# Decode attention on one core: taking the maximum of a head across partitions with two fp32 TensorE products instead of VectorE copies and transposes

## Chip, cores and metric

The kernel runs on one core of one Trainium2 chip. The metric is the time of one execution on the device in microseconds (us).

## The reference

Two attention blocks decode one token each. A has 32 heads with their own K and V of 32768 keys; B has 32 query heads over 8 K/V heads and looks at the last 4096 keys only. Cut to A, which is nearly all of the work:

```python
# A: x (1,1,512), k_cache and v_cache (1,32,32768,128), all bf16
q = (x @ wq).reshape(B, Sq, H, Dh).transpose(0, 2, 1, 3)
scores = jnp.einsum("bhqd,bhkd->bhqk", q, k_cache) * (Dh ** -0.5)
p = softmax(scores, axis=-1)
o = jnp.einsum("bhqk,bhkd->bhqd", p, v_cache)
a = o.transpose(0, 2, 1, 3).reshape(B, Sq, H * Dh) @ wo
# ... B the same with a window; out = concatenate([a, b], axis=-1)
```

One head of A reads 8.39 MB of K and 8.39 MB of V. The core reads 570 MB in all, and each byte is used once.

## The kernel before

A head of A goes through five steps. TensorE transposes K in tiles of 128 keys (`psT`) and VectorE copies them to SBUF (`kt`). TensorE multiplies them with q, so that the 32768 scores of the head stand in one PSUM bank `S` of 128 partitions by 512 (in 16 of each 32 rows, 64 in all). The maximum of the bank is taken. ScalarE computes Exp with that maximum as its bias. TensorE transposes the result (`psPT`) and multiplies it with V (PV). SyncE issues the loads; each waits for the room that it fills.

The part that the change replaces is the maximum. It takes the maximum of each row, transposes the column of 128 maxima in 32x32 blocks, copies the four pieces to one partition, takes their maximum, copies it back to four partitions, transposes again and scales:

```python
def emit_stats(self, name, g):
    self.emit_S(self.pending.pop(0))
    # ... (cut: short names; W = 16 and HG = 1 for A)
    o = dve(lambda v: v.reduce_max(tr["in"][:, 0:1], self.S[:, :], axis=AXX), self.sdone, self.k_pool)
    o = dve(lambda v: v.transpose(tr["a"][:, :], tr["in"][:, :]), o)
    for c in range(STRIPS):
        x = dve(lambda v, c=c: v.tensor_copy(m4[0:1, W * c:W * c + W], tr["a"][32 * c:32 * c + 1, 0:W]), o)
    o = dve(lambda v: v.reduce_max(t["mr"][0:1, :], m4[0:1, 0:4 * W].rearrange("p (k h) -> p h k", h=HG), axis=AXX), x)
    for c in range(STRIPS):
        x = dve(lambda v, c=c: v.tensor_copy(
            t["b"][32 * c:32 * c + 1, 0:W].rearrange("p (k h) -> p k h", k=KC),
            t["mr"][0:1, :].unsqueeze(1).to_broadcast([1, KC, HG])), o)
    o = dve(lambda v: v.transpose(t["cm"][:, :], t["b"][:, :]), x)
    o = dve(lambda v: v.tensor_scalar_mul(t["nb"][:, k:k + 1], t["cm"][:, 0:1], -self.SCALE), o, to="act")
    self.sread = self.op("act", lambda s: s.activation(
        out=self.psb[:, :], in_=self.S[:, :], func=ACTF.Exp, bias=t["nb"][:, k:k + 1], scale=self.SCALE,
        accum_out=t["oc"][k][:, DH:DH + 1]), o, self.psread, to="pe")
```

`load_v(g)` goes out when PV of head g-1 has ended (one V buffer). `load_k(g+1)` goes out when the first half of head g's K has been transposed (K has one and a half buffers). Both are on one queue, in this order. The output matrix Wo is loaded last, into the room of the last K: B's in two pieces, A's in four of 12, 10, 6 and 4 tiles of 128x512.

```python
WO_CUTS = {"A": (0, 12, 22, 28, 32), "B": (0, 16, 32)}

def emit_proj(self):
    # B's projection: 32 products into S
    for part in range(len(self.WO_CUTS["B"]) - 1):
        o = self.proj_part("B", part, ...)
    strips = self.op("dve", lambda v: v.tensor_copy(self.pb[:, :], self.S[:, :]), o)
    # A's projection: 32 products, a piece at a time, each piece after its landing
    for part in range(len(self.WO_CUTS["A"]) - 1):
        last = self.proj_part("A", part, lambda a: (self.PT[0:1, :], None, a == 0, a == 31))
        if part == 0:     # the fp32 product that adds B's four strips
            o = self.op("pe", lambda e: e.matmul(self.ACC[0:1, :], lhsT=self.e32[:, 0:1], rhs=self.pb[:, :], ...))
            self.store("B", self.ACC, 512, o)
    self.store("A", self.PT, 0, last)
```

## Time and profile before

| | kernel before |
|---|---|
| time, median of 3 runs | 1331.03 us (1330.01 to 1332.43) |
| load queue busy, of 16 engines' span | 99.4% |
| TensorE / VectorE / ScalarE busy | 72% / 61% / 4% |
| one head of A in the loop | 38.8 us |
| row maximum to Exp, in a head | 3.11 us |
| TensorE waits for Exp, all heads | 127.9 us |
| TensorE waits for K of A | 123.8 us |

First the load queue and the chain of work that ended last, from the page. The line "q1" gives packets, MB and the share of 16 engines' span.

```profile
q1 hardware_dynamic: 12628, 570.43, 99.4%
...
DMA 68%; PE 28%; DVE 3%; issue 0%; ACT 0%; SPq 0%
```

The queue is busy from end to end. The chain says 68% DMA and 28% PE. The PE share is no second limit: it lies between the landing of one K and the issue of the next K, and the V load is moving in that time. The Trainium skill ("Perfetto Trace Analysis", Identifying the Most-Contended Engine) says to optimize the most contended engine first, and to judge DMA by the HBM bandwidth used rather than by busy time. Here the DMA engines move 429 GB/s on average and the load queue is busy for 99.4% of the span, and the change does not touch it.

Now one head's maximum, from the timeline (columns: start in us, duration in us, engine, line, operation, output from inputs, forms, count; in brackets the idle time of the engine before it).

```profile
648.98 0.69 DVE L522 TENSOR_REDUCE tr_in<-psS 128x1 f32<-128x512 f32 x1 [0.51 <-PE psS L505]
649.71 0.21 DVE L523 STREAM_TRANSPOSE tr_a<-tr_in 128x32 f32<-128x32 f32 x1
649.95 0.69 DVE L525 COPY m<-tr_a 1x16 f32<-1x16 f32 x4
650.68 0.21 DVE L526 TENSOR_REDUCE mr_A<-m 1x1 f32<-1x64 f32 x1
650.92 0.70 DVE L528 COPY b_A<-mr_A 1x16 f32<-1x16 f32 x4
651.66 0.21 DVE L531 STREAM_TRANSPOSE cm_A<-b_A 128x32 f32<-128x32 f32 x1
651.90 0.15 DVE L532 TENSOR_SCALAR nb_A<-cm_A 128x1 f32<-128x1 f32 x1
652.09 0.69 ACT L533 ACTIVATE psb<-psS,nb_A 128x512 bf16<-128x512 f32 x1 [35.86 <-DVE nb_A L532]
...
652.92 0.61 PE L543 MATMUL psPT<-ident,psb 128*128 128x128 bf16 x4 [4.00 <-ACT psb L533]
...
659.65 0.33 SPq L284 DMA_DIRECT2D vbuf<-in_A_v_cache_dram  x1
...
666.20 6.24 PE L483 MATMUL psT<-ident,kbuf 128*128 128x128 bf16 x64 [4.52 <-DMA kbuf<-in_A_k_cache_dram]
```

Row maximum at 648.98, Exp at 652.09: 3.11 us. TensorE sat idle for 4.00 us until Exp was done, and again for 4.52 us until K landed. The V load was issued at 659.65, while the K issued at 637.91 landed at 666.15 only: 6.5 us of the queue were left when V joined it.

Last, the end of the run, from the timeline.

```profile
1308.15 6.09 PE L571 MATMUL psACC<-vbuf,ptsb 128*4 128x512 bf16 x64 [0.69 <-ACT ptsb L546]
...
1317.15 3.29 PE L627 MATMUL psS<-kbuf,oz_B 128*1 128x512 bf16 x32
...
1320.27 2.75 PE L627 MATMUL psPT<-kbuf,oz_A 128*1 128x512 bf16 x12
...
1323.71 4.48 PE L627 MATMUL psPT<-kbuf,oz_A 128*1 128x512 bf16 x20
...
1328.23 0.68 DVE L633 CAST out_sb<-psPT 1x512 bf16<-1x512 f32 x1 [3.64 <-PE psPT L627]
```

PV of the last head, B's projection, 12 products of A's, the fp32 product (left out here), 20 more of A's, and the copy for the store follow each other without a wait for a load. A's last piece of Wo landed at 1325.27.

### The profile page before, as it was taken

The numbers are of one execution on the slowest core, as the hardware profiler recorded it, in microseconds if no ns is written. First come the engines' busy times: TensorE is split into PE (matmuls) and PEld (weight loads), VectorE is DVE, ScalarE is ACT, GpSimd is POOL, SyncE is SP. The second block draws the span as 40 slices with busy tenths as digits, with TensorE's granted clock in tenths as the row PEclk, the third lists the DMA queues.
The fourth block names the chain that finished last, engine by engine and source line by source line (L and its number), as shares of the span: only waits on it lengthen the run. The fifth ranks groups of instructions, "written<-read, shape, count | busy, mean of one in ns | idle before, by whom it ended". The sixth has DMA issues, their size and how long they took to land.

```text
span 1330.5 us, 28787 instructions
## 1 busy us (share of the span) xinstructions
PE 953.2 (72%) x13274; PEld 668.9 (50%) x13274; DVE 805.0 (61%) x1661; ACT 54.8 (4%) x167; POOL 2.0 (0%) x15
## 2 busy tenths in 40 slices
PE   3756677686767778676687867668787667868777
PEld 3544445554444555444455544446554444555452
DVE  2655566765556676555667655566765556676573
ACT  0000000000000000000000000000000000000000
POOL 0000000000000000000000000000000000000000
PEclk9868788887788888778889878888987888888788
DMA  9999999999999999999999999999999999999997
GB/s 394 429 438 429 437 428 439 431 422 439 418 435 433 437 428 431 431 439 431 433 430 439 431 433 430 439 431 433 432 437 430 435 431 428 439 435 431 428 435 322
DMA packets 12932, 570.66 MB, mean 429 GB/s; under 512 B 1522, under 2 KB 1524, under 8 KB 1780
## 3 DMA queue, kind: packets, MB, share of 16 engines
q1 hardware_dynamic: 12628, 570.43, 99.4%
q8 instruction: 12, 0.20, 0.1%
q10 hardware_dynamic: 288, 0.00, 0.0%
q14 instruction: 4, 0.03, 0.0%
HBM read 570.43 MB, written 0.00 MB: 429 GB/s over the span
## 4 chain that ended last, share of the span: by engine, by line
DMA 68%; PE 28%; DVE 3%; issue 0%; ACT 0%; SPq 0%
DMA kbuf<-in_A_k_cache_dram 65%; PE psT L483 23%; PE psS L505 3%; DMA kbuf<-in_B_k_cache_dram 3%; DVE kt L486 3%; PE psACC L571 1%; PE psPT L627 1%; PE psS L627 0%; DVE oc_A L587 0%; ACT psb L533 0%; PE psPT L543 0%; DVE tr_in L522 0%; DVE b_A L528 0%; DVE m L525 0%; SPq L284 0%
## 5 line engine op out<-in xcount | busy, mean ns | idle before, releaser
L486 DVE COPY kt<-psT 128x1024 bf16<-128x1024 bf16 x1056 | 655.3, 684 | 203.0 <-PE psT L483 201.4
L483 PE MATMUL psT<-ident,kbuf 128*128 128x128 bf16 x8448 | 577.7, 234 | 135.8 <-DMA kbuf<-in_A_k_cache_dram 123.8
L483 PEld LDWEIGHTS psT<-ident,kbuf 128*128 128x128 bf16 x8448 | 538.3, 106 | 227.8 <-DMA kbuf<-in_A_k_cache_dram 131.9
L571 PE MATMUL psACC<-vbuf,ptsb 128*4 128x512 bf16 (+1 forms) x2112 | 188.5, 534 | 22.8 <-ACT ptsb L546 22.0
L505 PE MATMUL psS<-kt,qw 128*32 128x512 bf16 x2048 | 157.6, 385 | 15.5 <-DVE kt L486 15.5
L585 DVE TENSOR_SCALAR oc_A<-psACC,hot_A 128x128 f32<-128x128 f32 x32 | 11.2, 351 | 255.5 <-PE psG L598 255.5
L571 PEld LDWEIGHTS psACC<-vbuf,ptsb 128*4 128x4 bf16 (+1 forms) x2112 | 60.8, 111 | 141.9 <-issue 96.1
L543 PE MATMUL psPT<-ident,psb 128*128 128x128 bf16 x136 | 20.5, 305 | 127.9 <-ACT psb L533 127.9
L543 PEld LDWEIGHTS psPT<-ident,psb 128*128 128x128 bf16 x136 | 11.7, 130 | 137.6 <-ACT psb L533 137.4
L533 ACT ACTIVATE psb<-psS,nb_A 128x512 bf16<-128x512 f32 x32 | 22.0, 687 | 1169.7 <-DVE nb_A L532 1169.7
L505 PEld LDWEIGHTS psS<-kt,qw 128*32 128x32 bf16 x2048 | 34.0, 95 | 58.0 <-DVE kt L486 31.4
L598 PE MATMUL psG<-oc_A,hw 128*32 128x128 f32 (+1 forms) x128 | 19.3, 227 | 52.3 <-DVE oc_A L587 52.3
L598 PEld LDWEIGHTS psG<-oc_A,hw 128*32 128x32 f32 x128 | 11.4, 109 | 62.4 <-DVE oc_A L587 55.0
L587 DVE SCALAR_TENSOR_TENSOR oc_A<-psACC,hot_A,oc_A 128x128 f32<-128x128 f32 x96 | 33.7, 351 | 3.4
L522 DVE TENSOR_REDUCE tr_in<-psS 128x1 f32<-128x512 f32 x34 | 23.5, 692 | 17.1 <-PE psS L505 17.1
L525 DVE COPY m<-tr_a 1x16 f32<-1x16 f32 (+1 forms) x136 | 22.3, 164 | 2.6
L528 DVE COPY b_A<-mr_A 1x16 f32<-1x16 f32 x128 | 21.1, 165 | 2.4
L546 ACT ACTIVATE ptsb<-psPT 128x512 bf16<-128x512 bf16 x34 | 20.3, 597 | 32.3 <-PE psPT L543 32.3
L439 PE MATMUL psACC<-x_B,vbuf 128*128 128x1 bf16 x128 | 3.6, 165 | 13.4 <-DMA x_B<-in_B_x_dram 13.4
L439 PEld LDWEIGHTS psACC<-x_B,vbuf 128*128 128x128 bf16 x128 | 3.5, 104 | 13.4 <-DMA x_B<-in_B_x_dram 13.4
L446 DVE CAST qz<-psACC 128x32 bf16<-128x32 f32 x1 | 0.2, 192 | 12.9 <-PE psACC L439 12.9
L523 DVE STREAM_TRANSPOSE tr_a<-tr_in 128x32 f32<-128x32 f32 x34 | 7.2, 212 | 1.2
(66 smaller groups left out, 87.5 us busy)
## 6 DMA issues: line engine op xcount, KB each, us to landing
kbuf<-in_B_k_cache_dram SPq DMA_DIRECT2D x2, 4096.0 KB, 32.7
vbuf<-in_B_v_cache_dram SPq DMA_DIRECT2D x2, 4096.0 KB, 23.7
kbuf<-in_A_k_cache_dram SPq DMA_DIRECT2D x2, 4096.0 KB, 22.7
vbuf<-in_B_wq_dram SPq DMA_DIRECT2D x1, 4096.0 KB, 12.3
vbuf<-in_A_wq_dram SPq DMA_DIRECT2D x1, 4096.0 KB, 32.5
kbuf<-in_B_wo_dram SPq DMA_DIRECT2D x2, 2048.0 KB, 31.8
kbuf<-in_A_wo_dram SPq DMA_DIRECT2D x1, 1536.0 KB, 27.5
kbuf<-in_A_wo_dram SPq DMA_DIRECT2D x1, 1280.0 KB, 30.2
```

What stands on the lines that cost most here:

```text
L483: inst = e.transpose(T[:, 128 * k:128 * k + 128], src[:, DH * k:DH * k + DH], self.ident[:, :])
L486: self.copies.append(self.op("dve", lambda v: v.tensor_copy(KT[:, :], T[:, :]), o, to="pe"))
L505: inst = e.matmul(self.S[32 * c:32 * c + 32, :], lhsT=win, rhs=self.kt[(bb + c // 2) % NKT][:, 512 * (c % 2):512 * (c % 2) + 512], start=b ...
L522: o = dve(lambda v: v.reduce_max(tr["in"][:, 0:1], self.S[:, :], axis=AXX), self.sdone, self.k_pool)
L525: x = dve(lambda v, c=c: v.tensor_copy(m4[0:1, W * c:W * c + W], tr["a"][32 * c:32 * c + 1, 0:W]), o)
L528: x = dve(lambda v, c=c: v.tensor_copy(t["b"][32 * c:32 * c + 1, 0:W].rearrange("p (k h) -> p k h", k=KC), t["mr"][0:1, :].unsqueeze(1).to ...
L533: self.sread = self.op("act", lambda s: s.activation(out=self.psb[:, :], in_=self.S[:, :], func=ACTF.Exp, bias=t["nb"][:, k:k + 1], scale= ...
L543: inst = e.transpose(PT[:, 128 * jj:128 * jj + 128], self.psb[:, 128 * jj:128 * jj + 128], self.ident[:, :])
L546: self.ptread = self.op("act", lambda s: s.activation(out=self.ptsb[:, :], in_=PT[:, 0:512], func=ACTF.Copy), self.psread, to="pe")
L571: inst = e.matmul(acc[32 * c:32 * c + rows, 0:512], lhsT=lhsT, rhs=rhs, start=begin, stop=end, tile_position=(0, 32 * c), skip_group_check ...
L587: o = self.op("dve", lambda v, src=src, hot=hot: v.scalar_tensor_tensor(out=oc, in0=src, scalar=hot, in1=oc, op0=ALU.mult, op1=ALU.add), p ...
L598: return self.op("pe", lambda e: e.matmul(self.G[0:32, c0 + c:c0 + c2], lhsT=win, rhs=t["oc"][g % 2][:, c:c2], start=False, stop=True, ski ...
```

## The change

The intent: the maximum should cross the partitions by two products. The first has the column of 128 row maxima as its stationary operand and a constant matrix `rows64` (ones that pick rows 32s to 32s+15) as the moving one, and lays 64 maxima in one row of PSUM. VectorE takes the maximum of the row. The second multiplies this one value with a row of 128 times -SCALE, so that the scaled value stands on all partitions. Twelve small VectorE operations of each head of A go (two transposes, eight copies, a maximum and a scaling), and two products, a maximum and a copy come. B keeps the old way.

```diff
@@ alloc, constants (cut) @@
+        self.rows64 = sb("rows64", [128, 64], F32)
+        self.nscale = sb("nscale", [1, 128], F32)
+        # ... two memsets and four copies fill them once
@@ emit_stats @@
-        o = dve(lambda v: v.reduce_max(tr["in"][:, 0:1], self.S[:, :], axis=AXX), self.sdone, self.k_pool)
+        o = dve(lambda v: v.reduce_max(tr["in"][:, 0:1], self.S[:, :], axis=AXX), self.sdone, self.k_pool,
+                to="pe" if name == "A" else None)
+        if name == "A":
+            o = self.op("pe", lambda e: e.matmul(self.ACC[0:1, 0:64], lhsT=tr["in"][:, 0:1], rhs=self.rows64[:, :],
+                                                 start=True, stop=True, skip_group_check=True),
+                        o, self.accread, self.k_sel, to="dve")
+            o = dve(lambda v: v.reduce_max(t["mr"][0:1, :], self.ACC[0:1, 0:64], axis=AXX), o, to="pe")
+            o = self.op("pe", lambda e: e.matmul(self.ACC[:, 64:65], lhsT=self.nscale[:, :], rhs=t["mr"][0:1, :],
+                                                 start=True, stop=True, skip_group_check=True), o, to="dve")
+            o = dve(lambda v: v.tensor_copy(t["nb"][:, k:k + 1], self.ACC[:, 64:65]), o, to="act")
+            self.sread = self.op("act", ...)      # Exp as before
+            return
         o = dve(lambda v: v.transpose(tr["a"][:, :], tr["in"][:, :]), o)
```

More of the change, by code (lines that the diff above doesn't have):

```diff
@@ L405, in constants @@
         pool(lambda g: g.memset(self.spread[:, :, :], 0.0))
+        pool(lambda g: g.memset(self.rows64[:, :], 0.0))
+        pool(lambda g: g.memset(self.nscale[:, :], -self.SCALE))
         for n in ("B", "A"):
@@ L426, in constants @@
             dve(lambda v, t=t, HG=HG: v.tensor_copy(t["hsel"][:, 32:32 + HG], t["lh"][:, :]), lh, self.k_pool)
+        for s in range(STRIPS):
+            rows = slice(32 * s, 32 * s + 32)
+            dve(lambda v, rows=rows, s=s: v.tensor_copy(self.rows64[rows, 16 * s:16 * s + 16],
+                                                        self.ident[rows, 32 * s:32 * s + 16]), self.k_pool)
         for dq in range(4):
@@ L521, in emit_stats @@
         dve = lambda fn, *deps, **k: self.op("dve", fn, *deps, **k)
-        o = dve(lambda v: v.reduce_max(tr["in"][:, 0:1], self.S[:, :], axis=AXX), self.sdone, self.k_pool)
+        o = dve(lambda v: v.reduce_max(tr["in"][:, 0:1], self.S[:, :], axis=AXX), self.sdone, self.k_pool,
[8 more added lines that the diff above has]
+            o = dve(lambda v: v.tensor_copy(t["nb"][:, k:k + 1], self.ACC[:, 64:65]), o, to="act")
+            self.sread = self.op("act", lambda s: s.activation(
+                out=self.psb[:, :], in_=self.S[:, :], func=ACTF.Exp, bias=t["nb"][:, k:k + 1], scale=self.SCALE,
+                accum_out=t["oc"][k][:, DH:DH + 1]), o, self.psread, to="pe")
+            return
         o = dve(lambda v: v.transpose(tr["a"][:, :], tr["in"][:, :]), o)
```

## The prediction

> **What bounds the kernel now.** The load queue, for nearly all of the 1330.5 us span. The queue table gives 99.4% of 16 engines. In the table of stretches the DMA share is 1.00 from 100 to 1280 us, at 430 to 434 GB/s; a head of A moves 16.8 MB, which at 432 GB/s takes the 38.8 us that the timeline shows as the period of a head. The chain of waits says the same (68% DMA). Its 28% PE is no second bound: it lies between a K load's landing and the next K's issue, while the V load is moving. From the timeline around 640 to 690 us: V is issued at 659.65 while the K issued at 637.91 is in flight until 666.15 (6.5 us of queue left); K is issued at 677.69 while that V runs until about 684.8 (some 7 us left). The queue never runs dry.
>
> **The change, per head of A.** From the start of the row maximum to the start of Exp the trace shows 3.11 us (648.98 to 652.09) (timeline), of which the row maximum is 0.69. The new chain keeps the row maximum (0.69), and adds two fp32 products, a maximum of 64 out of PSUM (about 0.21) and a one-column copy (0.19, as the PSUM casts of oz). A small fp32 product in this trace (the one-column psG gather) is busy for 0.20 us, and a crossing VectorE to TensorE and back costs about 0.05 + 0.07 us more: estimate 0.35 each. New chain about 1.8 us: 1.3 us less per head, 41 us over 32 heads; VectorE loses about 55 us of 805 busy. The added set-up hides in the 13 us wait for x.
>
> **How much is on the critical path.** In heads 0 to 30, nothing: PV ends, and V is issued, 1.3 us earlier into a queue with 6 us of work in it. The 41 us become a longer wait of TensorE for K. Only the last head counts: after 1283 us the chain runs through VectorE's copies, the row maximum (1302.91), Exp (1306.02), PV (1308.15 to 1314.07), the projections and the store. There 1.3 us should come through. It has a floor: the last piece of Wo lands at about 1325.3, and four products (0.22 us apart) must follow, against their end at 1328.23 now, so at most about 1.9 us. A side effect may add: the Trainium skill ("TensorE: Matmul & The Clock Gate", Part 1) says the array clock is halved after an idle window of about 3.4 us. This trace agrees: TensorE waits 4.0 us for Exp in each head, and the granted clock is 0.50 in the PV after it. A wait of 2.7 us may keep full clock in some heads; in the loop that is worthless too.
>
> **Prediction:** 1329.5 us, range 1327.6 to 1331.3 (the kernel's own runs spread over 2.4 us). Faster by over 2%: 0.01; within 2%: 0.98; slower by over 2%: 0.01.
>
> **What would show each step right.** Row maximum to Exp: 1.8 us instead of 3.11. TensorE's wait for K: up from 124 us by about 40. DMA share still 1.00 and 430 to 434 GB/s in the loop. V issued about 1.3 us earlier after its K's issue, but landing 26.3 us after issue instead of 25. The period of a head unchanged. The last store 1 to 2 us earlier.
>
> **What would make it wrong.** Queue gaps that the DMA share hides (loads limited by their issue): then up to 40 us would come off. Or the fp32 products take over 1 us each. Or a TensorE clock that falls at another moment in the last head, costing or giving 1 to 2 us.

## The result

| | before | after |
|---|---|---|
| time, median of 6 runs | 1331.85 us (1330.01 to 1332.43) | 1331.40 us (1329.82 to 1331.99) |
| ratio | | 0.9996, 95% interval 0.9983 to 1.0009 |
| row maximum to Exp | 3.11 us | 1.93 us |
| TensorE waits for Exp | 127.9 us | 34.0 us |
| TensorE waits for K of A | 123.8 us | 162.1 us |
| VectorE busy | 805.0 us | 751.7 us |
| queue left when V is issued, mean of 31 heads | 5.7 us | 7.0 us |

A ratio is the mean time of one kernel's fast runs over the mean of the other's in the same rounds, so it is not quite the ratio of the medians. "Queue left" is worked out from the trace: the landing of the K load ahead less the issue of the V load. The change is within the noise, 0.04% with an interval that holds 1. The forecast of "within 2%" holds; the range, 1327.6 to 1331.3, misses the median by 0.1 us, and the centre by 1.9.

The queue and the chain of work after, from the page:

```profile
q1 hardware_dynamic: 12628, 570.43, 99.3%
...
DMA 69%; PE 28%; DVE 2%; issue 0%; ACT 0%; SPq 0%
```

The new chain, from the timeline of a head at the same place:

```profile
649.86 0.69 DVE L530 TENSOR_REDUCE tr_in<-psS 128x1 f32<-128x512 f32 x1 [0.51 <-PE psS L513]
...
650.61 0.27 PE L534 MATMUL psACC<-rows,tr_in 128*1 128x64 f32 x2 [0.80 <-DVE tr_in L530]
650.92 0.21 DVE L537 TENSOR_REDUCE mr_A<-psACC 1x1 f32<-1x64 f32 x1 [0.36 <-PE psACC L534]
...
651.18 0.38 PE L538 MATMUL psACC<-mr_A,nscale 1*128 1x1 f32 x2 [0.30 <-DVE mr_A L537]
651.60 0.16 DVE L540 COPY nb_A<-psACC 128x1 f32<-128x1 f32 x1 [0.47 <-PE psACC L538]
651.79 0.69 ACT L541 ACTIVATE psb<-psS,nb_A 128x512 bf16<-128x512 f32 x1 [37.49 <-DVE nb_A L540]
...
652.62 0.40 PE L565 MATMUL psPT<-ident,psb 128*128 128x128 bf16 x4 [1.06 <-ACT psb L541]
...
665.78 5.92 PE L491 MATMUL psT<-ident,kbuf 128*128 128x128 bf16 x64 [4.90 <-DMA kbuf<-in_A_k_cache_dram]
```

The chain became 1.18 us shorter (estimated: 1.3), with 0.27 and 0.38 us for the two products. TensorE now idles 1.06 us before `psPT` instead of 4.00, but 4.90 us before K instead of 4.52. The waits say the same of all heads, before (first fence) and after (second fence); columns: engine, output and line that waited, on what, us in all, times, longest.

```profile
PE psPT L543 <- ACT psb L533: 127.9, 32, 4.0
PE psT L483 <- DMA kbuf<-in_A_k_cache_dram: 123.8, 31, 11.3
```

```profile
PE psT L491 <- DMA kbuf<-in_A_k_cache_dram: 162.1, 31, 11.8
...
PE psPT L565 <- ACT psb L541: 34.0, 32, 1.1
...
PE psACC L534 <- DVE tr_in L530: 25.5, 32, 0.8
...
DVE nb_A L540 <- PE psACC L538: 15.0, 32, 0.5
...
PE psPT L649 <- DMA kbuf<-in_A_wo_dram: 2.7, 1, 2.7
```

94 us of waiting for Exp went (127.9 - 34.0). 35 us of this are now waits for the products' operands (25.5 + 9.7), and 21 us are the products themselves (8.7 + 12.1 us busy). The other 38 us, 1.18 us a head, are what the chain became shorter, and they came back as longer waits for K (162.1 - 123.8). The loop did what was predicted. The last line is new: a wait of 2.7 us for `in_A_wo`, once, at the end of the run.

```profile
1305.05 5.32 PE L593 MATMUL psACC<-vbuf,ptsb 128*4 128x512 bf16 x64 [0.69 <-ACT ptsb L568]
...
1313.24 2.08 PE L649 MATMUL psS<-kbuf,oz_B 128*1 128x512 bf16 x32
...
1317.98 4.41 PE L649 MATMUL psPT<-kbuf,oz_A 128*1 128x512 bf16 x12 [2.65 <-DMA kbuf<-in_A_wo_dram]
...
1323.11 4.48 PE L649 MATMUL psPT<-kbuf,oz_A 128*1 128x512 bf16 x20
...
1327.63 0.68 DVE L655 CAST out_sb<-psPT 1x512 bf16<-1x512 f32 x1 [3.64 <-PE psPT L649]
```

Here is where the forecast gain of the tail went. PV begins and ends early, but at 1315.3, after B's projection, TensorE stands until A's first piece of Wo lands (1317.93). The 12 products after it take 4.41 us instead of 2.75. The table of stretches shows why (columns: us, busy us of PE, PEld, DVE, ACT, POOL with counts, granted clock, DMA share, GB/s):

```profile
1316.00:1318.00 2.00, 0.02 (x1) 0.03 (x2) 0.07 (x1) 0.00 (x0) 0.00 (x0) 1.00 1.01 425
1318.00:1320.00 2.00, 2.00 (x7) 0.65 (x8) 0.00 (x0) 0.00 (x0) 0.00 (x0) 0.73 0.99 401
1320.00:1322.00 2.00, 2.00 (x6) 0.64 (x5) 0.00 (x0) 0.00 (x0) 0.00 (x0) 0.50 0.60 247
```

After the wait the clock fell to 0.50. The Trainium skill ("TensorE: Matmul & The Clock Gate", Part 1) describes this halving after an idle window of some 3.4 us; here a wait of 2.65 us inside such a window was enough, with the clock at 1.00 during the wait and 0.50 from about 1318.9 on. (From 1315.50 to 1318.91 TensorE was busy for 0.93 us.) A second profile of the same kernel, e11 below, has the half clock in A's projection too:

```profile
1317.58 4.14 PE L649 MATMUL psPT<-kbuf,oz_A 128*1 128x512 bf16 x12 [1.82 <-DMA kbuf<-in_A_wo_dram]
```

But there the clock had already fallen at 1313.59, before the wait of 1.82 us, and it came back at 1320.42. So both profiles show the half clock in A's projection; that the wait brings it about holds for the first alone.

The load queues of two runs do not keep quite the same pace, so clock times of two profiles should not be subtracted. Counted from the landing of the last whole K load (head 30) instead, at 1247.47 and 1246.32:

| us after K of head 30 landed | before | after |
|---|---|---|
| Exp of the last head | 58.5 | 56.8 |
| its PV begins / ends | 60.7 / 66.8 | 58.7 / 64.1 |
| B's projection ends | 73.0 | 69.0 |
| A's first piece of Wo landed | 71.6 | 71.6 |
| A's projection begins | 72.8 | 71.7 |
| A's projection ends, copy for the store | 80.8 | 81.3 |

At the end of B's projection the changed kernel leads by 4.0 us. These come from the shorter chains of heads 30 and 31 (K of head 31 had landed when TensorE came to it, so both count, not the last alone) and from more time at full clock in PV and in B's projection. Of the lead, 1.1 us are left when A's projection begins: TensorE has to wait for the first piece. None is left at its end: the half clock costs more than the rest.

### The profile page after: what moved, and what is told of

It reads as the page before. It is cut to its first block, busy times and chain, and to the rows that moved or that the text cites. A ratio compares the mean times of both kernels' runs of the same rounds, so it can differ in the third digit from the quotient of the medians.

```text
span 1329.9 us, 28729 instructions
## 1 busy us (share of the span) xinstructions
PE 970.0 (73%) x13402; PEld 682.1 (51%) x13402; DVE 751.7 (57%) x1345; ACT 54.8 (4%) x167; POOL 2.3 (0%) x17
## 4 chain that ended last, share of the span: by engine, by line
DMA 69%; PE 28%; DVE 2%; issue 0%; ACT 0%; SPq 0%
DMA kbuf<-in_A_k_cache_dram 64%; PE psT L491 24%; PE psS L513 4%; DMA kbuf<-in_B_k_cache_dram 3%; DMA kbuf<-in_A_wo_dram 2%; DVE kt L494 1%; PE psPT L649 1%; PE psACC L593 0%; SPq L286 0%; DVE oc_A L609 0%; PE psACC L667 0%; PE psPT L565 0%; ACT psb L541 0%; DVE tr_in L530 0%; DVE out_sb L655 0%
## 5 line engine op out<-in xcount | busy, mean ns | idle before, releaser
L491 PE MATMUL psT<-ident,kbuf 128*128 128x128 bf16 x8448 | 582.9, 235 | 174.1 <-DMA kbuf<-in_A_k_cache_dram 162.1
L593 PE MATMUL psACC<-vbuf,ptsb 128*4 128x512 bf16 (+1 forms) x2112 | 181.0, 517 | 22.8 <-ACT ptsb L568 22.0
L565 PE MATMUL psPT<-ident,psb 128*128 128x128 bf16 x136 | 17.4, 268 | 34.0 <-ACT psb L541 34.0
L534 PE MATMUL psACC<-rows,tr_in 128*1 128x64 f32 x64 | 8.7, 217 | 25.5 <-DVE tr_in L530 25.5
L534 PEld LDWEIGHTS psACC<-rows,tr_in 128*1 128x1 f32 x64 | 2.7, 81 | 35.1 <-DVE tr_in L530 35.1
L538 PE MATMUL psACC<-mr_A,nscale 1*128 1x1 f32 x64 | 12.1, 256 | 9.7 <-DVE mr_A L537 9.7
L538 PEld LDWEIGHTS psACC<-mr_A,nscale 1*128 1x128 f32 x64 | 9.4, 182 | 15.7 <-DVE mr_A L537 15.7
L540 DVE COPY nb_A<-psACC 128x1 f32<-128x1 f32 x32 | 5.1, 158 | 15.0 <-PE psACC L538 15.0
```

The lines of the kernel that those rows point to most:

```text
L491: inst = e.transpose(T[:, 128 * k:128 * k + 128], src[:, DH * k:DH * k + DH], self.ident[:, :])
L538: o = self.op("pe", lambda e: e.matmul(self.ACC[:, 64:65], lhsT=self.nscale[:, :], rhs=t["mr"][0:1, :], start=True, stop=True, skip_group_ ...
L565: inst = e.transpose(PT[:, 128 * jj:128 * jj + 128], self.psb[:, 128 * jj:128 * jj + 128], self.ident[:, :])
L593: inst = e.matmul(acc[32 * c:32 * c + rows, 0:512], lhsT=lhsT, rhs=rhs, start=begin, stop=end, tile_position=(0, 32 * c), skip_group_check ...
```

## The experiments

Two theories were at hand. Theory 1: the load queue bounds the loop, so the shorter chain is worth nothing there, and at the end its gain is lost to the landing of Wo. Rival: the length of the chain does count, and the gain is eaten by a cost of the two products (semaphores, fp32 passes, clock). The runs of a group shared a chip and the runs of the kernel before, whose medians there were 1331.71, 1331.57 and 1331.87 us.

### Does the length of the chain count in the loop? (e1, e2)

```diff
+            # (cut: the row maximum no longer signals TensorE, the last clear does)
+            for i in range(6):        # e2: 20
+                o = dve(lambda v: v.memset(self.pb[:, :], 0.0), o, to="pe" if i == 5 else None)
             o = self.op("pe", lambda e: e.matmul(self.ACC[0:1, 0:64], ...
```

> The changed kernel with six dummy VectorE clears (about 0.5 us each) between the row maximum and the first product of every head of A: row maximum to Exp grows from 1.93 to about 5.0 us, longer than before the change (3.1 us). Theory (the load queue bounds the loop, and a head has slack): the loop keeps its pace of about 38.8 us a head, TensorE's wait for K falls from 162 us to about 70 us, and only the last head pays: 0 to 2 us over the changed kernel, 1331 to 1334 us. Rival (the length of the chain counts in every head, and the gain was lost to some cost of the two products): 32 x 3.1 us more, about 1430 us.

Measured: 1351.47 us (1342.62 to 1353.71), 20 us over the kernel before: neither theory's number. The dose was wrong first: each clear waits for the one before it, and takes 0.66 us from start to start, not 0.5.

```profile
658.89 0.69 DVE L530 TENSOR_REDUCE tr_in<-psS 128x1 f32<-128x512 f32 x1 [0.51 <-PE psS L513]
659.76 0.48 DVE L534 MEMSET pb<- 128x512 f32 x1 [0.17 <-DVE tr_in L530]
660.41 0.48 DVE L534 MEMSET pb<- 128x512 f32 x1 [0.17 <-DVE pb L534]
...
665.08 0.69 ACT L542 ACTIVATE psb<-psS,nb_A 128x512 bf16<-128x512 f32 x1 [39.24 <-DVE nb_A L541]
...
667.21 6.26 PE L594 MATMUL psACC<-vbuf,ptsb 128*4 128x512 bf16 x64 [0.69 <-ACT ptsb L569]
...
673.51 0.33 SPq L286 DMA_DIRECT2D vbuf<-in_A_v_cache_dram  x1
...
704.17 4.86 PE L594 MATMUL psACC<-vbuf,ptsb 128*4 128x512 bf16 x64 [0.69 <-ACT ptsb L569]
```

Row maximum to Exp is 6.19 us (658.89 to 665.08), 4.3 more than in the changed kernel. Over 32 heads this adds 136 us of work to the chain, of which 20 reached the time; so most of it is hidden, as theory 1 says, but not all. The trace shows which part is not. With PV longer at half clock in every second head (mean granted clock 0.57 against 0.74, 6.26 us against 4.86), V is issued with only 1.24 us of queue left in that head (673.51; the K load ahead landed at 674.75), and it lands at 695.24, 20.5 us after that K. A load of 8.39 MB behind a full queue lands 19.35 us after the one before it (666.15 to 685.50 in the kernel before). So 1.1 us is lost in every second head, 17 us in all. By these numbers V must be issued some 2.4 us before the queue runs out (an estimate: 1.24 + 1.1); the 5.7 us left before the change and 7.0 after are well over it. I had counted the queue as safe down to zero.

> The same with twenty clears, about 10.3 us a head. Theory: TensorE's wait for K (5.2 us a head in the changed kernel) is used up, and the half clock that follows that wait (about 2 us a head) too; then the rest counts: 31 x (10.3 - 5.2 - 2.1 to 0) us and some 10 us of the last head, so 1430 to 1500 us, with the DMA share in the loop clearly under 1.00. If the loop's slack were only imagined, e1 would have shown it; if slack is larger than I think (the queue holds more), the time stays near 1340.

Measured: 1573.58 us, 242 us over the kernel before; the added chain was 13.5 us a head (row maximum to Exp 15.4 us), by the same 0.66 us. The queue's share fell to 85.3%, and V went out 3 to 7 us after the queue had run dry, landing 21.8 us after its issue, which is 2.5 us more than the 19.35. Over 31 heads, 242 us are 7.8 us a head, so about 5.7 us of the 13.5 were hidden. That is the slack of the loop in the changed kernel, close to its mean wait for K of 5.2 us (162.1 us over 31). The expectation of 1430 to 1500 us was for 10.3 us a head.

### What is the change worth where loads are not the limit? (e3, e4)

```diff
-            self.load(self.kbuf[:, w * lo:w * lo + 2 * w], src, ...)
+            n = 2 * w if g < 3 else w
+            self.load(self.kbuf[:, w * lo:w * lo + n], src[:, 0:n], ...)
@@ load_v: the same halving @@
```

Their outputs are wrong, which doesn't matter for the times.

> The kernel before, but each load of K and V of heads 3 to 31 (K but for head 31) brings only its first half, so the rest is stale and the result is wrong on purpose. This takes the load queue's bound away. Theory: the loop falls to the pace of its own chain of work: 38.8 us less the 4.0 us wait for K and about 2 us of half clock, some 33 us a head, 1140 to 1220 us in all. DMA share in the loop 0.5 to 0.65.

> The changed kernel with the same halved loads. Theory: now the shorter chain counts in each head: 1.2 us (3.11 to 1.93) plus some of the clock, 28 x 1.2 to 1.6 us, so 32 to 48 us less than e3. Rival (the products on TensorE cost as much as they save, so the change is worth nothing anywhere): within 5 us of e3.

Measured: 1202.93 us for the kernel before and 1150.47 us for the changed one, with halved loads. The difference is 52.5 us or 4.4%, more than the 32 to 48 expected. The queue has room in both, by the page's queue lines, e3 first:

```profile
q1 hardware_dynamic: 12628, 331.36, 66.8%
...
q1 hardware_dynamic: 12628, 331.36, 69.9%
```

With that much room the 1.18 us of each head arrive (at most 32 x 1.18 = 38 us; the first three heads still have whole loads). The other 15 us or so fit the clock: the mean granted clock is 0.879 in e3 and 0.909 in e4, the products of PV are busy for 184.5 us instead of 191.2, and the transposes of K for 524.2 instead of 533.4. So the rival falls: the products cost nothing that cancels the gain. In the real kernel the gain is there and has nowhere to go.

### Where did the end lose it? (e5 to e8)

e5 and e6 take A's Wo out of the way: each of its four loads brings one tile only (wrong result).

```diff
+        a1 = a0 + 1 if name == "A" else a1      # in load_wo
```

> The kernel before, but each of the four loads of A's Wo brings one of its tiles only (0.5 MB instead of 4 MB in all; wrong result on purpose). Theory (before the change the last head's chain ends the run, and Wo is there in time): TensorE came to A's projection at 1320.3 us and the first piece had landed at 1319.1, so nothing is gained: within 1 us of the kernel before. Rival (Wo's landing ends both runs): 3 us or more faster.

> The changed kernel with the same small loads of A's Wo. Theory (the last head's gain is lost to Wo's landing, which makes TensorE wait 2.65 us and then run at half clock): the wait goes, 12 products take 2.75 us instead of 4.41, and the run is 3 to 4.5 us shorter than the changed kernel, about 1327.3 us, also 3 to 4.5 us shorter than e5. Rival (the gain is lost elsewhere, or was never there): within 1 us of the changed kernel.

Measured: e5 1331.96 us (ratio to the kernel before 1.0002), e6 1327.31 us (0.9965, interval 0.9949 to 0.9982). Theory 1 holds in both: the kernel before gains nothing from an early Wo, the changed kernel gains its 4 us, and the two now differ by 4.65 us. The end of e6, from the timeline:

```profile
1314.78 2.75 PE L650 MATMUL psPT<-kbuf,oz_A 128*1 128x512 bf16 x12
...
1322.74 0.68 DVE L656 CAST out_sb<-psPT 1x512 bf16<-1x512 f32 x1 [3.64 <-PE psPT L650]
```

No wait, and 2.75 us for the 12 products. (PV of e6 waited 1.38 us for V, which landed at 1304.07: the landing of the last V is the next floor.)

e7 leaves Wo alone and keeps TensorE busy while it waits.

```diff
+        def busy(e):      # ahead of A's projection, into a bank that nothing reads
+            for _ in range(10):
+                inst = e.matmul(self.T[1][:, :], lhsT=self.ident[:, :], rhs=self.kt[0][:, 0:512], ...)
+            return inst
+        self.op("pe", busy)
```

> The changed kernel with ten dummy bf16 products of 512 columns (about 0.22 us each) in the wait for A's Wo, into a bank that nothing reads. Theory (half clock after the wait is a part of the loss): the clock stays at 1.00 there, the first 12 products of A's projection take about 2.75 us instead of 4.41, and the run is 1 to 2 us shorter than the changed kernel. Rival (the landing of Wo alone ends the run): within 0.5 us of it.

Measured: 1330.82 us, ratio to the kernel before 0.9990 (0.9973 to 1.0007). This is 0.6 us under the changed kernel's first median and 0.8 under its later one: between the two theories, and too small to be told from noise. The trace shows both halves of a trade: the 12 products were at full clock again (2.75 us), but the dummies ran at half clock themselves until 1317.41 and held TensorE until 1318.76, when the piece had landed at 1317.53.

e8 was meant as the better version: A's Wo in six pieces, the fp32 product ahead of A's projection, and six dummy products.

> The changed kernel with a tail built for Wo's landing: A's Wo in six pieces (6, 6, 6, 6, 5, 3 tiles) instead of four, the fp32 product for B put ahead of A's projection, six dummy products after it. Theory: the work left after the last landing (about 1324.1 us) is three products, a copy and the store, so the last copy starts at about 1325.2 instead of 1327.63: 2 to 3 us shorter than the changed kernel, about 1328.8 us. Rival: more pieces cost more than they bring, same or slower.

Measured: 1330.72 us (1329.44 to 1332.40), no gain to speak of; a miss. In its trace the first piece landed at 1315.87, and TensorE came to it at 1321.05: the fp32 product (1.86 us at half clock) and the dummies stood in the way. The idea of the pieces was buried under my additions, so it was tried alone.

### The pieces alone (e9, e10, e11)

```diff
-    WO_CUTS = {"A": (0, 12, 22, 28, 32), "B": (0, 16, 32)}
+    WO_CUTS = {"A": (0, 6, 12, 18, 24, 29, 32), "B": (0, 16, 32)}
```

> The changed kernel with A's Wo in six pieces (6, 6, 6, 6, 5, 3 tiles) instead of four (12, 10, 6, 4), and nothing else: no dummy products, the fp32 product for B stays after the first piece. Theory (in the changed kernel TensorE waits for the large first piece and then has all 32 products of A's projection still ahead, in part at half clock): TensorE starts at about 1316 us instead of 1318, its last product ends at about 1325.5 us instead of 1327.6, so 1.5 to 2.5 us shorter than e11, about 1329.3 us. Rival (what ends the run is the last landing, whatever the pieces): within 0.7 us of e11.

> The kernel before with the same six pieces. Theory: TensorE reaches A's projection at about 1320 us, when four of the six pieces have landed, and has 32 products and the fp32 one to do without a wait: nothing gained, within 0.7 us of the kernel before. Rival (smaller pieces pay by themselves): as much shorter as e9 is.

> The changed kernel itself, unedited, timed beside the other two so that differences of a microsecond can be read. Theory: 0.3 to 1.0 us shorter than the kernel before, which is what its trace showed at the last store (1327.63 against 1328.23 us).

| five rounds each | median, us | range | ratio to before (95%) |
|---|---|---|---|
| before (9 runs) | 1331.87 | 1330.25 to 1332.53 | |
| e10: before, six pieces | 1331.22 | 1329.24 to 1331.79 | 0.9995 (0.9981 to 1.0008) |
| e11: the changed kernel | 1331.58 | 1330.02 to 1331.71 | 0.9998 (0.9984 to 1.0012) |
| e9: the changed kernel, six pieces | 1329.38 | 1329.25 to 1329.52 | 0.9984 (0.9970 to 0.9997) |

The pieces bring 2.2 us to the changed kernel and nothing that can be read to the one before, and only with them does the change show at all. Counted from the landing of K of head 30 again, in these profiles:

| us after K of head 30 landed | e10 (before, six) | e11 (after) | e6 (after, small Wo) | e9 (after, six) |
|---|---|---|---|---|
| B's projection ends | 73.8 | 69.9 | 69.0 | 69.0 |
| A's first piece landed | 69.8 | 71.6 | 68.3 | 69.8 |
| A's projection begins | 73.7 | 71.7 | 68.9 | 69.9 |
| copy for the store | 81.6 | 81.0 | 76.8 | 78.9 |

The copy was at 80.8, 81.3 and 81.6 in the three profiles with the old chain (before, e5, e10) and at 81.3 and 81.0 in the two of the changed kernel: less than 0.1 us between the two means. e9's end, from the timeline:

```profile
1314.18 1.03 PE L649 MATMUL psS<-kbuf,oz_B 128*1 128x512 bf16 x16 [0.59 <-DMA kbuf<-in_B_wo_dram]
...
1316.06 1.46 PE L649 MATMUL psPT<-kbuf,oz_A 128*1 128x512 bf16 x6 [0.85 <-DMA kbuf<-in_A_wo_dram]
...
1321.67 3.42 PE L649 MATMUL psPT<-kbuf,oz_A 128*1 128x512 bf16 x14 [0.40 <-DMA kbuf<-in_A_wo_dram]
...
1325.12 0.68 DVE L655 CAST out_sb<-psPT 1x512 bf16<-1x512 f32 x1 [6.03 <-PE psPT L649]
```

TensorE follows the landings with short waits of 0.85 and 0.40 us and stays at full clock (1.00 in each stretch from 1316 to 1324 us). The last piece landed at 1324.09 and the last copy starts 1.03 us later, so hardly more than this can be had at the end while the queue is full. e9 is the fastest correct version, by 0.16% over the kernel before.

## Why the prediction was right or wrong

- Right: "In heads 0 to 30, nothing". The loop stayed at 38.8 us a head (38.80 before, 38.76 after, from the first and last landing of K), the wait for K grew by 38 us, V was issued earlier by 1.2 us in the mean and landed 26.3 us after its issue instead of 25.1 (medians), as written. e3 and e4 show that the same change is worth 4.4% where the queue is not full. The detail is a little off: head 30 counts too, because K of head 31 is there early.
- Right in size: the chain, 1.93 us against 1.8 estimated. The two products took 0.27 and 0.38 us.
- Wrong: "There 1.3 us should come through. It has a floor: the last piece of Wo lands at about 1325.3, and four products (0.22 us apart) must follow". The term of the sum that was mis-sized is the gain of the end, taken as 1.5 us; it measured 0.3 to 0.5 us in the medians and under 0.1 us in the profiles. The runs showed two things that the sum did not have. First, the floor was drawn from the last piece alone, but TensorE takes the pieces in order. The first, of 12 tiles, landed at 1317.93, which left 32 products and the fp32 one to do after it, 7.9 us at full clock (2.75 + 1.02 + 4.48, less overlaps, as in e6 from 1314.78 to 1322.70). In the kernel before, TensorE came to that piece 1.2 us after its landing; 1.2 us was all the lead it could use there (1.7 and 2.0 in e5 and e10, the other two profiles of the old chain), though 4.0 us had been won. This cap alone would have left about what was forecast. Second, the sum ran A's projection at its old pace. In the three profiles with the old chain it took 7.9 us, all at full clock; in the two of the changed kernel it took 9.6 and 9.3 us, in part at half clock. Those 1.4 to 1.7 us cancel most or all of the lead that was left. e6 shows the lead without the landing and the half clock (4.65 us under e5), e9 with smaller pieces (2.2 us under e11, at full clock too).
- Wrong too: the base. I took 1331.03, the median of three runs; further runs brought the medians 1331.85, 1331.71, 1331.57 and 1331.87. This is 0.5 to 0.8 us of the 1.9 by which the centre missed. A range of plus or minus 1.9 us was too narrow for a base that three runs with a spread of 2.4 us had fixed.
- The half clock was foreseen in the loop and as a risk "in the last head", but with no number in the sum. In the first pair of profiles it was a cost in A's projection and a gain in PV and B's projection. In the loop it did not go: the mean granted clock of a PV was 0.58 to 0.68 before and 0.56 to 0.77 after (heads 1 to 31). And the "0.50 in the PV after it" is true of a part of PV: in the head shown the clock fell at 650.99, 2.1 us into the wait, and was back at 657.81, while PV ran from 654.22 to 659.60.
- Open: the split of the end into landing and clock is read from traces; no run changed one alone (e7 changed both). Where the clock falls is partly luck: the stretches of the clock's record (see the last section) in which it could fall had TensorE busy for 1.78 us in the first profile of the changed kernel and 1.70 in e6, and it stayed; in e11 they had 1.63, and it fell. And the kernel before spreads over 2 us from run to run while e9 spreads over 0.3; the phase of the clock at the end is a likely cause, not a shown one.

## What to carry to other kernels

When one queue is full from end to end, a shorter chain inside the loop only moves the wait; test it by halving the loads of both versions, which shows at once whether the gain exists and where it goes. Draw the floor of the tail from every landing in the order in which the engine takes them, with the work still behind each, and not from the last landing alone. Give the clock a term of its own too: here it was worth 1.4 to 1.7 us in the last 32 products. When a chain gets shorter, cut the last loads smaller, so that the engine meets them piece by piece and neither waits long nor loses its clock.

## What the Trainium skill lacked or had wrong

- "TensorE: Matmul & The Clock Gate", Part 1, names "≥1 idle window (~3.4µs)" for the fall to half clock. The window need not be idle: in the changed kernel a wait of 2.65 us was enough, and in e7 the clock fell at 1314.0 us after 3.4 us in which the profile shows TensorE busy for 1.74 us. In all 13 traces the clock changed only at the end of whole stretches of 3.41 us. Of 3325 such stretches at full clock, 757 were followed by the fall: all that had TensorE busy for less than 1.6 us and, with one exception in each run, none that had it busy for more than 1.75 us. The exception lies near 38 us, where products with a moving operand of a single column (Wq) fill the stretch (3.35 us of them in the kernel before), so their busy time seems not to count.
- "DMA: Bandwidth & Descriptors", Latency and other measured facts, gives about 0.6 us to the first byte for loads issued from SyncE. The same section also speaks of a fixed cost of about 2 us for a DMA, and that is the nearer figure here. For keeping a queue full the runs give more than the 0.6 us: an 8.39 MB load issued 1.24 us before the queue ran out (e1) still cost 1.1 us, so about 2.4 us from the issue (estimate); with the queue dry (e2) a load took 21.8 us from issue to landing, against 19.35 from one landing to the next behind a full queue.
- No page that I read gives the cost of a small fp32 product between two VectorE operations. Here the 128x64 one took 0.27 us and the 1x1 one with 128 stationary columns 0.38 us at full clock, and from the end of one VectorE operation to the start of the next it was 0.37 and 0.47 us.
- "VectorE: DVE Perf Modes", Why tensor_reduce can't reduce along partition axis, names GpSimd alone for a maximum across partitions. Two fp32 products on TensorE, with a VectorE maximum of 64 values between them and a copy after, did it here in 1.24 us, from the end of the row maximum (650.55) to the start of Exp (651.79), against 2.42 us for the twelve VectorE operations; GpSimd was not tried.
